# Other places for attention units, a fold, operand buffers, PSUM banks and the last group's turns in a fused attention and MLP kernel

## The chip, the cores and the metric

The kernel runs on one core of a Trainium2 chip. Its time is the device time of one execution in microseconds (us). A core has five engines that run side by side, each in the order of its own instructions: TensorE (PE) multiplies matrices into PSUM banks, VectorE (DVE) and ScalarE (ACT) work on elements, GpSimd (POOL) is hardly used here, SyncE (SP) issues the DMA transfers. They wait for each other by semaphores.

## The reference, cut to what matters

```python
# 8 batches x 576 positions = 4608 tokens, 8 heads of 64; everything is fp32
for each chunk of 64 tokens, each batch and head:
    s = q @ k.T / 8;  s = exp(s - max(s));  p = s / sum(s);  x = p @ v
# x: [4608, 512]
a = x @ w1;  b = x @ w2                 # moe:  512 -> 1024
y = ((a * b) @ w3) @ w_out              #       1024 -> 1024 -> 512
h = y @ w_in                            # moe2: 512 -> 2048
g = max(h, 0) + alpha * min(h, 0)
out = g @ w_out2                        #       2048 -> 512
```

## The kernel before, in words

Every fp32 operand is kept as two rounded halves, HI and LO, and each product is three passes of matmuls (LO x HI, HI x HI, HI x LO). A 128x512 matmul starts every 227 ns in a full stretch.

**First products, blocks b = 0 to 8 of 512 tokens.** A hand-written list starts the kernel (blocks 0 and 1, up to about 139 us). Then comes the loop over `b = 2..8` and `f = 0..7`. A step f has two half-slots of twelve matmuls: `a` into one bank of a pair, copied by ACT, and `b` into the other, multiplied by VectorE with that copy. The product `a*b` goes to DRAM (`g_dram`). Between the half-slots stand the pieces of two attention units of 256 tokens each, for the next block: `unit_parts` puts four pieces of a unit (scores with the row maximum; exponentials, sum and scaling; transposes of the probabilities with their copy `pt` by ACT; product with `v` and the halves of `x`) after the half-slots that the tuple `places` names. In blocks 2 to 7 there are also calls of `convert()`: it splits a piece of a weight into its halves on ACT and VectorE (for moe2 further pieces `wm` are formed and stored). A converted piece of `w3` is later multiplied with `w_out` (`fold`, twelve matmuls into `wc`), so that moe's last two products become one. The order on TensorE is that of the program; on the other engines a scheduler sets it within limits.

**Last product of moe.** Five groups n of two half-blocks of tokens (the first one, s = 4, is half as wide). Each is a Winograd form of Strassen's scheme: seven products o0 to o6 of quarter operands in place of eight. `araw` tiles are read back from DRAM; VectorE and ACT form sums and the halves `op`, in a ring of buffer pairs named in `OPS`; TensorE multiplies them into banks, ACT and VectorE combine the results into `y`. Towards the end of this stage `load_y` and `operand(o)` prepare the operands `yo` of moe2 in the order `ORDER`, at the places that `EARLY` names.

**First product of moe2.** 18 turns of 14 slots, six matmuls a slot, seven products again, each for two column pieces i = 0, 1 (function `both`). A turn uses `a` (two banks) for products 4, 3, 0 and 6 and banks `b`, `c` for 5, 2 and 1. ACT copies the running sum out of `a` at three points (`keep`: p1, u2, v), VectorE adds `b` or `c`, ACT and VectorE apply the leaky step, and the result `r` goes to DRAM. All these tiles share one ring of work buffers, `tmp`. At the last turn of a group s each product's operand is replaced by the next group's (`operand`, one ACT cast and one addition).

**Last product of moe2.** Five groups as in moe. The last group's results are transposed on TensorE, copied by ACT into rows `o`, and stored by SP.

Of the kernel before, what the change touches and what calls it, by code (L numbers as in the profile page):

```python
# [18 lines left out]
P = 128  # L19
TB = 512  # L20
# [33 lines left out]
PAIRS = [(1, 2), (3, 4), (5, 6), (7, 8)]  # L54
# [23 lines left out]
def tile_attention_moe_moe(ctx: ExitStack, tc: tile.TileContext, qkv: bass.AP, w12: bass.AP,  # L78
# [177 lines left out]
    def convert():  # L256

        i = ahead[0]
        if i >= len(conv):
            return  # L260
        ahead[0] = i + 1
        while folds and folds[0] <= i - 2:
            fold(folds.pop(0))
        if conv[i][0] == "m":
            second_weight(i)
            if i % 2:
                combined_weight(i)
        else:
            convert_a(i)
            convert_b(i)  # L270
            convert_a(i + 1)
            convert_c(i)
            convert_d(i)
            convert_e(i)
            folds.append(i)
# [170 lines left out]
    def add(out, x, y, op=ALU.add):  # L446
        vector.tensor_tensor(out=out, in0=x, in1=y, op=op)

    ORDER = (4, 3, 5, 0, 2, 6, 1)
    y_op, ys = {}, {}  # L450

    def load_y(s):
# [115 lines left out]
            moe_weight[at] = [parts[:, a, i] for a in (HI, LO)]  # L568

    CONVERSIONS = {4: 7, 5: 7, 6: 6, 7: 6, 8: 2}  # L570
    pinned[0] = True
    for b in range(2, NB):
        parts = {}
        if b + 1 < NB:
            for i, places in enumerate(((0, 1, 4, 6), (8, 9, 12, 13)) if b < 4 else ((0, 1, 6, 8), (4, 5, 10, 12))):
                parts.update(unit_parts(2 * (b + 1) + i, places))
        for f in range(NF1):
            pa, pb = (bank(n) for n in ("cd" if sets % 2 else "ab"))
            sets += 1
            proj1(b, f, 0, pa)  # L580
            a = tmp("a")
            scalar.copy(a, pa)
            parts.get(2 * f, lambda: None)()
            proj1(b, f, 1, pb)
            product(b, f, a, pb)
            parts.get(2 * f + 1, lambda: None)()
            n = CONVERSIONS.get(b, 0)
            for _ in range(1 + (f in (3, 4)) if b < 4 else n * (f + 1) // NF1 - n * f // NF1 if b < NB - 1 else f < n):
                convert()
            if (b, f) == (3, NF1 - 1):  # L590
                while folds:
                    fold(folds.pop(0))
                load_unit(11)
            if b == NB - 1:
                for at in LOADS[f]:
                    moe_weights(*at)

    EARLY = {2: (-1,), 3: ORDER[:4], 4: ORDER[4:]}
    turns = Counter()

    def copied(out, x):
# [32 lines left out]


    RAWS, SUMS = ("raw0", "raw1", "raw2", "s31"), ("s28", "s29", "s30")
    OPS = (("s16", "s17"), ("s18", "s19"), ("s20", "s21"), ("s22", "s23"))
    NM = NF1 // 4
    groups = (len(PAIRS),) + tuple(range(len(PAIRS)))
    reads = [(s, q, m) for s in groups  # L640
# [10 lines left out]
    for n, s in enumerate(groups):  # L651
        w = wide[s]
        x5, x4, c11, u2 = (post[:, i, :, :w] for i in range(4))
        (b0, c0), (b1, c1) = ((b, 0) for b in PAIRS[s]) if s < len(PAIRS) else ((0, 0), (0, HW))

        def keep_y(b, c, k, x, w=w):
            nc.sync.dma_start(out=y_dram[b][:, k:k + 2, c:c + w], in_=x)

        qa, qc = ("p23", "att") if n % 2 == 0 else ("att", "p23")
        p5, p4 = pair(qa, "q")[:, :, :w], [bank(q)[:, :w] for q in "ab"]  # L660
        sums = []
        for m in range(NM):
            a21, a22 = raw(s, 2, m), raw(s, 3, m)
            sm = slot(cycle("sum", SUMS), "sum", F32)[:, :, :w]
            add(sm, a21, a22)
            sums.append(sm)
            o4 = spread(a22)
            o5 = spread(sm)
            ordered[0] = True
            for f in closing:  # L670
                f()
            closing = []
            multiply(o4, m, 1, p4, m == 0, m == NM - 1)
            multiply(o5, m, 0, p5, m == 0, False)
        p7, p1 = pair(qc, "q")[:, :, :w], [bank(q)[:, :w] for q in "cd"]
        if n == len(PAIRS):
            weights(0, 0)
        for m in range(NM):
            a11, a21 = raw(s, 0, m), raw(s, 2, m)
            add(a21, a11, a21, ALU.subtract)  # L680
            o1 = spread(a11)
            o7 = spread(a21)
            if m == 0:
                for e in range(2):
                    copied(x4[:, e], p4[e])
                copied(x5, p5)
            multiply(o1, m, 4, p1, m == 0, False)
            multiply(o7, m, 2, p7, m == 0, m == NM - 1)
            add(sums[m], sums[m], a11, ALU.subtract)
            o6 = spread(sums[m])  # L690
            if m == 0:
                p6 = [bank(q)[:, :w] for q in "ab"]
            multiply(o6, m, 3, p6, m == 0, m == NM - 1)
        for e in range(2):
            copied(c11[:, e], p1[e])
        if n == len(PAIRS):
            weights(0, 1)
        for m in range(NM):
            a12 = raw(s, 1, m)
            multiply(spread(a12), m, 5, p1, False, m == NM - 1)  # L700
            add(sums[m], a12, sums[m], ALU.subtract)
            multiply(spread(sums[m]), m, 6, p5, False, m == NM - 1)
            if m == 0:
                for e in range(2):
                    add(u2[:, e], p6[e], c11[:, e])
                add(x5, u2, x5)
                add(x5, p7, x5)
                keep_y(b1, c1, 2, x5)
            else:
                add(x4, u2, x4)  # L710
                add(x4, p7, x4)
                keep_y(b1, c1, 0, x4)

        def close(c11=c11, u2=u2, p1=p1, p5=p5, b0=b0, c0=c0, keep_y=keep_y):
            for e in range(2):
                copied(c11[:, e], p1[e])
            keep_y(b0, c0, 0, c11)
            add(u2, p5, u2)
            keep_y(b0, c0, 2, u2)
        closing = [close]  # L720
        for o in EARLY.get(n, ()):
            load_y(0) if o < 0 else operand(o)
    close()
    ordered[0] = False
    for j in range(2, NJ // 2):
        weights(0, j)

    def products(s, j, o, ps, first, last):
        for k in range(2):
# [1 line left out]
                matmul(ps, weight[j, o][a][:, k * P:(k + 1) * P], y_op[s, o][m][:, k],  # L731
                       start=first and k + i == 0, stop=k == 1 and i == 2, skip_group_check=not (first and last))
        if j == NJ - 1 and s + 1 < len(wide):
            operand(o)
    def leaky(s, js, q, h, t):
        w, r = wide[s], tmp("r")[:, :h.shape[1]]
        scalar.activation(out=r, in_=h, func=AF.Relu)
# [14 lines left out]
    for turn, (s, j, jj) in enumerate(passes):  # L752
        if j == (2 if s else 4) and s + 1 < len(wide):
            load_y(s + 1)
        if turn in (0, 1):
            for k in range(2):
                weights(0, 2 * turn + 4 + k)
        a = [bank(n) for n in "ab"]
        p1, u2, v, b, c = ([None] * 2 for _ in range(5))

        def both(i, o, ps, first, last):
            w = wide[s]
            for n, k in enumerate(jj[i]):
                products(s, k, o, ps[:, n * w:(n + 1) * w], first and n == 0, last)

        def keep(name, i):
            t = tmp(name)
# [1 line left out]
            return t  # L769

        def second(i):
            which = (2 * turn + i) % 3
            bc = pair("att" if which == 0 else "p23", "bc") if which != 1 else None
            b[i], c[i] = (bc[:, h] for h in range(2)) if bc is not None else (bank(n) for n in "cd")
            both(i, 5, b[i], True, True)
            add(p1[i], p1[i], b[i])
            leaky(s, jj[i], 0, p1[i], p1[i])
# [1 line left out]
        for i in range(2):  # L779
            both(i, 4, a[i], True, False)  # L780
            p1[i] = keep("p1", i)
        second(0)
        for i in range(2):
            both(i, 3, a[i], False, False)
            u2[i] = keep("u2", i)
        second(1)
        for i in range(2):
            both(i, 0, a[i], False, False)
            v[i] = keep("v", i)
# [21 lines left out]
    def fetch(t, s, q, m):  # L811
        nc.sync.dma_start(out=t, in_=g2_dram[s, q, m])

    def turned(s, c, half, tag, t):

        w = wide[s]
        ps = pair(tag, "tr")
        for i in range(2):
            for e in range(4):
                transpose(ps[:, i, e * P:(e + 1) * P], c[e // 2][:, e % 2, (t + i) * P:(t + i + 1) * P], ident)  # L820
        for i in range(2):
            o = tmp("o")
            scalar.copy(o.rearrange("p (a g c) -> p g a c", a=4, c=32), ps[:, i].rearrange("p (g a c) -> p g a c", a=4, c=32))
            b, r = (PAIRS[s][half], 0) if w == TB else (0, half * w)
            r += b * TB + (t + i) * P
            nc.sync.dma_start(out=out[r:r + P, :], in_=o)

    def rows(s, quads, half, t):

# [17 lines left out]
    for s in range(len(wide)):  # L847
# [48 lines left out]
            copied(c11[:, e], p1[e])  # L896
        for m in range(NM):
            a12 = raw(s, 1, m)
            multiply(spread(a12), m, 5, p1, False, m == NM - 1)
            add(sums[m], a12, sums[m], ALU.subtract)  # L900
            multiply(spread(sums[m]), m, 6, p5, False, m == NM - 1)
            if m == 0:
                for e in range(2):
                    add(u2[:, e], p6[e], c11[:, e])
                add(x5, u2, x5)
            elif m == 1:
                add(x4, u2, x4)
            elif m == 2:
# [6 lines left out]
            add(u2, p5, u2)  # L915
        closing = [close]
        done = [lambda s=s, c=c, h=h, t=t: rows(s, c, h, t) for h, c in ((1, (x4, x5)), (0, (c11, u2))) for t in range(w // P)]
    close()
    for t in range(0, w // P, 2):
        for h, c, q in ((1, (x4, x5), qc), (0, (c11, u2), qa)):  # L920
            turned(s, c, h, q, t)


# [45 lines left out]
```

## Time and profile before

| | |
|---|---|
| median of 3 runs | 1429.05 us (1426.08 to 1432.37) |
| profiled execution | 1429.92 us |
| its span on the trace | 1428.1 us |
| mean granted TensorE clock | 0.998 of full speed |
| TensorE busy | 1379.2 us, 97% of the span |
| VectorE busy | 1088.6 us, 76% |
| ScalarE busy | 767.4 us, 54% |
| blocks 2 to 8 of the first products | about 139 to 546 us |
| moe's last product | 546 to 721 us |
| moe2's first product | 721 to 1076 us |
| moe2's last product, with the stores | 1076 to 1428 us |

TensorE is nearly always busy, so a reader looks for the pauses of TensorE and at what ended each of them: an engine that waits is shown with the time that it sat idle before an instruction and the instruction of another engine that released it.

### The profile page before, as it was taken

Reading aid. Unit: us, or ns where it says so; the run is one execution under the profiler, and the core shown is the slowest. Engines: PE = TensorE matmul, PEld = TensorE weight load, DVE = VectorE, ACT = ScalarE, POOL = GpSimd, SP = SyncE. Lnnn points to the kernel's source line nnn. Section 1 sums busy time; section 2 is a strip of 40 time slices with the busy share of each in tenths; the row PEclk is TensorE's granted clock in tenths of the full one; section 3 lists DMA queues with packets and bytes.
Section 4 is the critical chain, followed back from the end, with each engine's and each line's share of the span. In section 5 each row is a group of like instructions: output and inputs, shape, how many; then the busy total and the mean of one; then the engine's idle time right before and its main releaser. Section 6 shows DMA issues by size and latency. Waiting matters only on the chain.

```text
span 1428.1 us, 23134 instructions
## 1 busy us (share of the span) xinstructions
PE 1379.2 (97%) x8584; PEld 1149.2 (80%) x8584; DVE 1088.6 (76%) x1601; ACT 767.4 (54%) x1597; POOL 9.5 (1%) x22
## 2 busy tenths in 40 slices
PE   5899999999999999999999999999999999999998
PEld 4688778788778889887887787878898888888888
DVE  6889887778877856989855748575667879889785
ACT  6544454554554524454456767687765444444434
POOL 0000000000000000000000000000000000000020
PEclk9999999999999999999999999999999999999999
DMA  8654565699888855566984424332488563635452
GB/s 251 209 177 156 185 242 194 229 324 310 307 296 291 293 216 164 201 219 209 330 297 168 153 106 166 116 134 114 165 315 328 197 216 122 216 133 179 147 152 86
DMA packets 140673, 296.71 MB, mean 208 GB/s; under 512 B 14608, under 2 KB 62224, under 8 KB 140560
## 3 DMA queue, kind: packets, MB, share of 16 engines
q1 hardware_dynamic: 140048, 294.19, 59.7%
q8 instruction: 67, 1.10, 0.3%
q0 software_dynamic: 512, 1.05, 0.2%
q14 instruction: 46, 0.38, 0.1%
HBM read 182.98 MB, written 112.20 MB: 207 GB/s over the span
## 4 chain that ended last, share of the span: by engine, by line
PE 72%; DVE 12%; DMA 6%; ACT 6%; issue 3%; SPq 1%; ACTq 0%; DVEq 0%
PE b L124 15%; PE a L124 14%; PE q L124 14%; PE d L124 10%; PE c L124 9%; PE bc L124 6%; ACT e L70 4%; DVE m L70 3%; PE wc L124 3%; DVE p L70 2%; DMA raw<-in_w 1%; DMA yq<-y_dram 1%; DVE wm L70 1%; PE pa L124 1%; DMA araw<-g_dram 1%
## 5 line engine op out<-in xcount | busy, mean ns | idle before, releaser
L124 PE MATMUL q<-op,w 128*128 128x512 f32 (+1 forms) x960 | 211.8, 368 | 0.0
L124 PEld LDWEIGHTS q<-op,w 128*128 128x128 f32 x960 | 168.5, 189 | 29.9
L70 ACT CAST op<-araw 128x1024 fp32r<-128x1024 f32 (+1 forms) x120 | 115.4, 967 | 117.2 <-PE d L124 37.6
L70 DVE TENSOR_TENSOR op<-araw,op 128x1024 fp32r<-128x1024 f32 (+1 forms) x120 | 132.9, 1113 | 25.4 <-ACT op L70 24.9
L70 ACT CAST op<-sum 128x1024 fp32r<-128x1024 f32 (+1 forms) x90 | 87.0, 967 | 88.9 <-PE q L124 55.0
L70 DVE TENSOR_TENSOR op<-sum,op 128x1024 fp32r<-128x1024 f32 (+1 forms) x90 | 100.2, 1113 | 32.8 <-ACT op L70 32.2
L124 PE MATMUL b<-x,wa 128*128 128x512 f32 x432 | 110.0, 405 | 0.0
L124 PE MATMUL a<-yo,w 128*128 128x512 f32 (+1 forms) x438 | 103.1, 373 | 5.1 <-ACT p L70 3.2
L124 PE MATMUL a<-x,wa 128*128 128x512 f32 x432 | 104.5, 390 | 3.5 <-DVE x L70 3.5
L124 PE MATMUL d<-x,wa 128*128 128x512 f32 x432 | 105.2, 392 | 0.4 <-DVE wa L70 0.4
L124 PE MATMUL c<-x,wa 128*128 128x512 f32 x432 | 104.5, 390 | 0.0
L70 ACT ACTIVATE e<-sc,mx 128x64 f32<-128x64 f32 x288 | 86.0, 361 | 23.8 <-DVE mx L70 23.8
L124 PEld LDWEIGHTS a<-x,wa 128*128 128x128 f32 x432 | 80.7, 188 | 20.5 <-DVE x L70 3.8
L124 PEld LDWEIGHTS b<-x,wa 128*128 128x128 f32 x432 | 81.4, 193 | 17.8
L124 PEld LDWEIGHTS a<-yo,w 128*128 128x128 f32 x438 | 76.9, 188 | 22.2 <-ACT p L70 5.0
L124 PEld LDWEIGHTS c<-x,wa 128*128 128x128 f32 x432 | 80.9, 188 | 16.9
L124 PEld LDWEIGHTS d<-x,wa 128*128 128x128 f32 x432 | 80.2, 188 | 16.8 <-DVE wa L70 0.5
L124 PE MATMUL b<-yo,w 128*128 128x512 f32 (+1 forms) x402 | 91.8, 367 | 0.8 <-ACT t L70 0.8
L124 PE MATMUL c<-op,w 128*128 128x512 f32 (+1 forms) x345 | 89.7, 368 | 0.7 <-DVE op L70 0.7
L124 PE MATMUL bc<-yo,w 128*128 128x512 f32 (+1 forms) x408 | 90.1, 363 | 0.0
L124 PE MATMUL d<-op,w 128*128 128x512 f32 (+1 forms) x345 | 89.6, 368 | 0.0
L124 PE MATMUL a<-op,w 128*128 128x512 f32 (+1 forms) x315 | 81.9, 368 | 1.4 <-DVE op L70 1.4
(143 smaller groups left out, 2505.2 us busy)
## 6 DMA issues: line engine op xcount, KB each, us to landing
araw<-g_dram SPq DMA_DIRECT2D x120, 512.0 KB, 4.1
g_dram<-r SPq DMA_DIRECT2D x144, 256.0 KB, 2.0
w_dram<-wm SPq DMA_DIRECT2D x48, 512.0 KB, 4.6
w<-w_dram SPq DMA_DIRECT2D x48, 512.0 KB, 6.4
qk<-in_qkv SPq DMA_DIRECT2D x36, 512.0 KB, 6.0
g_dram<-a SPq DMA_DIRECT2D x72, 256.0 KB, 3.3
raw<-in_w2nd SPq DMA_DIRECT2D x32, 512.0 KB, 5.3
raw<-in_w SPq DMA_DIRECT2D x16, 512.0 KB, 4.3
```

Of the source, the lines that this page charges most:

```text
L70: ins = f(*args, **kw)
L124: ins = nc.tensor.matmul(*args, **kw)
```

## The change

- `convert()` makes a fold when two are outstanding, and only at a piece of `w3`; the last two folds come in block 4 (f = 0 and 1) rather than at the end of block 3, and the load of unit 11 after them.
- The places of the attention pieces are other ones in block 2 and in blocks 4 to 7.
- `ORDER` is (4, 5, 3, ...); the operands of moe2 are prepared at other points of the last two groups.
- `OPS` has six pairs of buffers, and four again in the last group.
- In moe2's first product, `a` takes banks a, b in even turns and c, d in odd ones; `b` and `c` take the same two pairs in every turn; product 5 of both pieces comes before product 3; an operand is replaced two calls of `both` later.
- In moe2's last group eight transposes (x5, x4) stand ahead of the last two multiplications, copies are divided between ACT and VectorE, and the stores between ACT's and SP's queues.

```diff
@@ convert
-        while folds and folds[0] <= i - 2:
-            fold(folds.pop(0))
         if conv[i][0] == "m":
...
         else:
+            if len(folds) > 1:
+                fold(folds.pop(0))
             convert_a(i)
@@
-    ORDER = (4, 3, 5, 0, 2, 6, 1)
+    ORDER = (4, 5, 3, 0, 2, 6, 1)
@@ loop over blocks
+    PLACES_OF = {2: ((0, 1, 5, 7), (9, 10, 13, 14)), 3: ((0, 1, 4, 6), (8, 9, 12, 13))}
-            for i, places in enumerate(((0, 1, 4, 6), (8, 9, 12, 13)) if b < 4 else ((0, 1, 6, 8), (4, 5, 10, 12))):
+            for i, places in enumerate(PLACES_OF.get(b, ((0, 1, 5, 7), (6, 8, 11, 13)))):
...
-            if (b, f) == (3, NF1 - 1):
-                while folds:
-                    fold(folds.pop(0))
-                load_unit(11)
+            if b == 4 and f < 2:
+                fold(folds.pop(0))
+                if f == 1:
+                    load_unit(11)
@@ moe's last product
-    EARLY = {2: (-1,), 3: ORDER[:4], 4: ORDER[4:]}
+    EARLY = {(3, 2, 0): (-1,), (3, 3, 0): ORDER[:1], (4, 1, 1): ORDER[1:2], (4, 2, 0): ORDER[2:3], (4, 2, 1): ORDER[3:4]}
-    OPS = (("s16", "s17"), ("s18", "s19"), ("s20", "s21"), ("s22", "s23"))
+    OPS = tuple((f"s{n}", f"s{n + 1}") for n in range(12, 24, 2))
+        def early(part, m):
+            for o in EARLY.get((n, part, m), ()):
+                load_y(0) if o < 0 else operand(o)
+        if n == len(PAIRS):
+            OPS = OPS[2:]
+            turns["op"] = 0
...
     close()
+    for o in ORDER[4:]:
+        operand(o)
@@ moe2's first product
         if j == NJ - 1 and s + 1 < len(wide):
-            operand(o)
+            late.append((calls[0] + 2, o))
...
-        a = [bank(n) for n in "ab"]
+        a = [bank(n) for n in ("ab", "cd")[turn % 2]]
...
+            while late and late[0][0] <= calls[0]:
+                operand(late.pop(0)[1])
+            calls[0] += 1
...
         def second(i):
-            which = (2 * turn + i) % 3
-            bc = pair("att" if which == 0 else "p23", "bc") if which != 1 else None
-            b[i], c[i] = (bc[:, h] for h in range(2)) if bc is not None else (bank(n) for n in "cd")
+            bc = pair(("att", "p23")[i], "bc")
+            b[i], c[i] = (bc[:, h] for h in range(2))
...
         second(0)
+        if s < len(PAIRS):
+            second(1)
         for i in range(2):
             both(i, 3, a[i], False, False)
             u2[i] = keep("u2", i)
-        second(1)
+        if s == len(PAIRS):
+            second(1)
@@ moe2's last group
+            final = s == len(PAIRS) and m == NM - 1
+            if not final:
+                multiply(o2, m, 5, p1, False, m == NM - 1)
...
+            if final:
+                tr = pair(qc, "tr")
+                rows1 = [tmp("o") for _ in range(2)]
+                turned(x5, 1, [tr[:, 0], tr[:, 1]], rows1)
+                turned(x4, 0, [bank(q) for q in "ab"], rows1)
+                stored(1, rows1)
+            multiply(o3, m, 6, p5, False, m == NM - 1)
+            if final:
+                multiply(o2, m, 5, p1, False, True)
...
+def turned(x, h, ps, os):     # 4 transposes, then one copy by ACT and one by VectorE
+def stored(half, os):
+        for t in range(2):
+            r = half * HW + t * P
+            (nc.sync if t else nc.scalar).dma_start(out=out[r:r + P, :], in_=os[t])
```

The first place is ACT in block 5, around unit 12's copy `pt` and unit 13's exponentials `e` (x16 stands for sixteen in a row). Before:

```order
L70 COPY a_4115<-a_4101 128x512
L70 CAST wm_4089<-t32_4080 128x512
L70 ACTIVATE m_4192<-raw_3944 128x512
L70 CAST wm_4085<-t14_4079 128x512
L70 ACTIVATE e_3855,sm_4153<-sc_4117,mx_4150 128x64 x16
L70 COPY a_4212<-c_4198 128x512
L70 COPY pt_4223<-pa_4214 128x1024
```

And after the change:

```order
L70 COPY a_4115<-a_4101 128x512
L70 CAST wm_4089<-t32_4080 128x512
L70 ACTIVATE m_4147<-raw_3944 128x512
L70 CAST wm_4085<-t14_4079 128x512
L70 COPY pt_4140<-pa_4131 128x1024
L70 COPY a_4167<-c_4153 128x512
L70 ACTIVATE m_4280<-raw_4071 128x512
L70 CAST wm_4300<-m_4073 128x512
L70 CAST wm_4304<-m_4147 128x256
L70 ACTIVATE e_3869,sm_4205<-sc_4169,mx_4202 128x64 x8
```

The copy stood behind the sixteen exponentials and one product copy; it now stands ahead of all of them.

The second place is VectorE in block 2, where the low half of a piece of `w3` is finished (`w3_2263` before, `w3_2198` now: the same piece) and unit 7's softmax is scaled (`e_1877`). Before:

```order
L70 TENSOR_SCALAR p_2301<-m_2264 128x512
L70 TENSOR_SCALAR m_2298<-m_2298 128x512
L70 TENSOR_TENSOR wm_2284<-m_2099,wm_2284 128x512
L70 SCALAR_TENSOR_TENSOR p_2301<-raw_2097,p_2301 128x512
L70 TENSOR_TENSOR m_2264<-m_2264,w3_2263 128x512
L70 TENSOR_TENSOR a_2320<-d_2307,a_2320 128x512
L70 TENSOR_TENSOR w3_2263<-m_2264,p_2301 128x512
```

And after the change:

```order
L70 TENSOR_TENSOR m_2199<-m_2199,w3_2198 128x512
L70 TENSOR_TENSOR w3_2198<-m_2199,p_2248 128x512
L70 TENSOR_SCALAR sm_2184<-sm_2184 128x16
L70 RECIPROCAL sm_2184<-sm_2184 128x16
L70 TENSOR_TENSOR a_2267<-d_2254,a_2267 128x512
L70 TENSOR_TENSOR e_1877<-e_1877,sm_2184 128x1024
L70 TENSOR_TENSOR t14_2314<-wf_2312 128x256
```

Before, the scaling of `e_1877` and the pieces of the combined weight stood ahead of the rows shown, 29 rows before the weight; now the weight is finished four rows ahead of that scaling.

The third place is ACT at the start of moe2's first product (its first turn, in the order of every turn). Before:

```order
L70 COPY p1_7550<-a_7542 128x512
L70 COPY p1_7558<-b_7543 128x512
L70 ACTIVATE r_7568<-p1_7550 128x512
L70 COPY u2_7579<-a_7542 128x512
L70 ACTIVATE p1_7550<-p1_7550 128x512
L70 COPY u2_7587<-b_7543 128x512
L70 ACTIVATE r_7598<-p1_7558 128x512
L70 COPY v_7609<-a_7542 128x512
```

And after the change:

```order
L70 COPY p1_7550<-a_7542 128x512
L70 COPY p1_7558<-b_7543 128x512
L70 ACTIVATE r_7568<-p1_7550 128x512
L70 ACTIVATE p1_7550<-p1_7550 128x512
L70 ACTIVATE r_7581<-p1_7558 128x512
L70 COPY u2_7592<-a_7542 128x512
L70 ACTIVATE p1_7558<-p1_7558 128x512
L70 COPY u2_7600<-b_7543 128x512
```

The first copy `u2` of a turn had one relu pass between it and the copies `p1`; it now has three, all over `p1` of the two column pieces.

## Rows read from the trace of the kernel before

**Rows 1.** The page, busy time of each engine, its share of the span, instructions.

```profile
PE 1379.2 (97%) x8584; PEld 1149.2 (80%) x8584; DVE 1088.6 (76%) x1601; ACT 767.4 (54%) x1597; POOL 9.5 (1%) x22
```

**Rows 2.** Waits of TensorE: for what, us in all, times, longest.

```profile
PE pa L124 <- ACT pt L70: 12.5, 7, 2.9
PE pa L129 <- DVE e L70: 7.2, 4, 3.4
...
PE wc L124 <- DVE w L70: 5.0, 2, 2.7
...
PE a L124 <- ACT p L70: 3.2, 3, 1.2
PE a L124 <- ACT t L70: 1.8, 4, 0.5
PE a L124 <- DVE op L70: 1.4, 1, 1.4
PE b L124 <- ACT t L70: 1.1, 4, 0.3
PE c L124 <- DVE op L70: 0.7, 1, 0.7
```

**Rows 3.** Windows: length, busy PE, PEld, DVE, ACT, POOL; clock, DMA share, GB/s.

```profile
195.00:215.00 20.00, 17.28 (x194) 13.72 (x192) 19.45 (x38) 9.55 (x16) 0.00 (x0) 1.00 0.83 274
...
360.00:380.00 20.00, 17.85 (x135) 14.50 (x134) 17.14 (x35) 13.18 (x47) 0.00 (x0) 0.91 0.92 320
420.00:440.00 20.00, 17.35 (x133) 14.13 (x133) 15.39 (x31) 13.01 (x46) 0.00 (x0) 0.91 0.75 263
```

**Rows 4.** Timeline of TensorE, blocks 5 and 6: start, us, line, operation, [idle before <-releaser].

```profile
372.45 1.16 PE L124 MATMUL pa<-pt,v 64*64 64x64 f32 x64 [2.15 <-ACT pt L70]
...
427.38 1.31 PE L124 MATMUL pa<-pt,v 64*64 64x64 f32 x64 [2.65 <-ACT pt L70]
```

**Rows 5.** Timeline of TensorE, block 2.

```profile
156.03 1.06 PE L129 MATMUL pa<-ident,e 128*128 128x128 f32 x8 [1.92 <-DVE e L70]
...
200.53 2.56 PE L124 MATMUL wc<-wo,w 128*128 128x512 f32 x10 [2.72 <-DVE w L70]
```

**Rows 6.** Timeline of ACT, block 5.

```profile
366.15 0.31 ACT L70 ACTIVATE e<-sc,mx 128x64 f32<-128x64 f32 x1 [2.37 <-DVE mx L70]
...
371.27 1.13 ACT L70 COPY pt<-pa 128x1024 f32<-128x1024 f32 x1
```

**Rows 7.** Timeline of VectorE, block 5.

```profile
371.53 1.23 DVE L70 TENSOR_TENSOR e<-e,sm 128x1024 f32<-128x1024 f32 x1
...
393.71 1.22 DVE L70 TENSOR_TENSOR x<-pa,x 128x1024 fp32r<-128x1024 f32 x1
```

**Rows 8.** Timeline of TensorE, block 5, unit 13.

```profile
357.13 1.16 PE L124 MATMUL sc<-qk 64*64 64x64 f32 x64
...
387.17 1.16 PE L124 MATMUL pa<-pt,v 64*64 64x64 f32 x64
```

**Rows 9.** Timeline of TensorE, moe2's first product: a boundary turn, a plain turn.

```profile
806.30 1.65 PE L124 MATMUL a<-yo,w 128*128 128x512 f32 x6 [0.90 <-ACT p L70]
...
825.49 1.52 PE L124 MATMUL a<-yo,w 128*128 128x512 f32 x6
826.85 1.52 PE L124 MATMUL b<-yo,w 128*128 128x512 f32 x6
```

**Rows 10.** Timeline of ACT, moe2's first product: a boundary turn, a plain turn.

```profile
794.62 1.06 ACT L70 CAST yo<-yq 128x1024 fp32r<-128x1024 f32 x1 [0.97 <-PE d L124]
...
805.66 0.59 ACT L70 COPY p<-a 128x512 f32<-128x512 f32 x1 [1.02 <-DMA g_dram<-r]
...
828.41 0.59 ACT L70 COPY u<-b 128x512 f32<-128x512 f32 x1 [0.24 <-PE b L124]
```

**Rows 11.** Timeline of TensorE and SP's queue, the end.

```profile
1421.17 2.10 PE L129 MATMUL tr<-ident,post 128*128 128x128 f32 x16
...
1422.86 1.90 SPq L826 DMA_DIRECT2D out<-o  x4
```

More of the change, by code (lines that the diff above doesn't have):

```diff
@@ L674, in tile_attention_moe_moe @@
             multiply(o5, m, 0, p5, m == 0, False)
+            early(1, m)
         p7, p1 = pair(qc, "q")[:, :, :w], [bank(q)[:, :w] for q in "cd"]
@@ L693, in tile_attention_moe_moe @@
             multiply(o6, m, 3, p6, m == 0, m == NM - 1)
+            early(2, m)
         for e in range(2):
@@ L712, in tile_attention_moe_moe @@
                 keep_y(b1, c1, 0, x4)
+            early(3, m)
         def close(c11=c11, u2=u2, p1=p1, p5=p5, b0=b0, c0=c0, keep_y=keep_y):
@@ L720, in tile_attention_moe_moe @@
         closing = [close]
-        for o in EARLY.get(n, ()):
-            load_y(0) if o < 0 else operand(o)
     close()
+    for o in ORDER[4:]:
+        operand(o)
     ordered[0] = False
@@ L726, in tile_attention_moe_moe @@
         weights(0, j)
+    late, calls = [], [0]
     def products(s, j, o, ps, first, last):
@@ L812, in fetch @@
         nc.sync.dma_start(out=t, in_=g2_dram[s, q, m])
[L814 to L826, printed above, removed]
+    def turned(x, h, ps, os):
+        for t in range(2):
+            for e in range(2):
+                n = (2 * h + e) * P
+                transpose(ps[t][:, n:n + P], x[:, e, t * P:(t + 1) * P], ident)
+        for t in range(2):
+            to, ps_t = (y.rearrange(f, a=4, c=32)[:, 2 * h:2 * h + 2]
+                        for y, f in ((os[t], "p (a g c) -> p g a c"), (ps[t], "p (g a c) -> p g a c")))
+            (vector.tensor_copy if t else scalar.copy)(to, ps_t)
+    def stored(half, os):
+        for t in range(2):
+            r = half * HW + t * P
+            (nc.sync if t else nc.scalar).dma_start(out=out[r:r + P, :], in_=os[t])
     def rows(s, quads, half, t):
@@ L898, in tile_attention_moe_moe @@
             a12 = raw(s, 1, m)
-            multiply(spread(a12), m, 5, p1, False, m == NM - 1)
+            o2 = spread(a12)
+            final = s == len(PAIRS) and m == NM - 1
+            if not final:
+                multiply(o2, m, 5, p1, False, m == NM - 1)
             add(sums[m], a12, sums[m], ALU.subtract)
-            multiply(spread(sums[m]), m, 6, p5, False, m == NM - 1)
+            o3 = spread(sums[m])
+            if final:
[7 more added lines that the diff above has]
+                multiply(o2, m, 5, p1, False, True)
             if m == 0:
@@ L905, in tile_attention_moe_moe @@
                 add(x5, u2, x5)
+            elif s == len(PAIRS):
+                if m == 1:
+                    add(x4, u2, x4)
+                    add(x5, p7, x5)
+                    add(x4, p7, x4)
             elif m == 1:
@@ L917, in tile_attention_moe_moe @@
         done = [lambda s=s, c=c, h=h, t=t: rows(s, c, h, t) for h, c in ((1, (x4, x5)), (0, (c11, u2))) for t in range(w // P)]
[L918 to L921, printed above, removed]
+    add(u2, p5, u2)
+    for e in range(2):
+        (vector.tensor_copy if e else scalar.copy)(c11[:, e], p1[e])
+    rows0 = [tmp("o") for _ in range(2)]
+    turned(u2, 1, [bank(q) for q in "ab"], rows0)
+    tr = pair(qc, "tr")
+    turned(c11, 0, [tr[:, 0], tr[:, 1]], rows0)
+    stored(0, rows0)
 def kernel(**inputs):
```

## The prediction

> **What bounds the kernel now.** I read the page's busy line first: TensorE is busy for 1379.2 us of the 1428.1 us span [rows 1]. The change neither adds nor removes matmuls, apart from eight transposes that go ahead of the last product, so the time can only move through TensorE's pauses. The waits of TensorE are therefore the second view [rows 2]. Most of the first three rows there belongs to the first 140 us, whose hand-written list is not touched. What the change can reach is: one wait of 1.92 us for a softmax [rows 5], both waits of a fold for its weight (5.0 us together) [rows 2], two waits of a values product for the copied probabilities (2.15 and 2.65 us) [rows 4], the two for `op` (1.4 and 0.7), and the rows for `p` and `t` (3.2, 1.8 and 1.1) that all lie in moe2's first product [rows 2]. The third view is the granted clock by stretch. The two 20 us windows that hold the waits of 2.15 and 2.65 us read 0.91, the one that holds a fold's wait reads 1.00 [rows 3]. At half speed for some 3.6 us of a window, 9% of 20 us is lost: 1.8 us more for each of the two.
>
> The Trainium skill, "TensorE: Matmul & The Clock Gate", section "HAM oscillation", has it that idle gaps take the clock down to half and that the penalty is paid again each time. Rows 3 and 4 agree for two waits, and the fold's wait of 2.72 us [rows 5], longer than either, cost no clock. So by the rule a pause costs itself or itself and 1.8 us, and which is not read from its length alone; I use this only for the price of new waits, below.
>
> **Part 1, attention units in blocks 4 to 7 (from 292 us to 502 us).** ACT runs in order. In block 5 the copy `pt` of unit 12 started at 371.27, behind the sixteen exponentials of unit 13, of which the first started at 366.15 [rows 6]; unit 12's values product then began at 372.45, late by 2.15 [rows 4]. The order shows the copy ahead of the exponentials now, since unit 12's turn comes one half-slot earlier and unit 13's scores two later. Unit 14 in block 6 is the same case. The gain is 2.15 + 2.65, and 2 x 1.8 of clock: 8.4 us.
>
> What is late next is the second unit of the block. Its probabilities were ready at 371.53 + 1.23 = 372.76 [rows 7], 14.5 us after its scores product ended (357.13 + 1.16) [rows 8]. From scores to turn there are now five half-slots of 2.72 us (twelve matmuls, two slots as in [rows 9]) and one values product of 1.16, 14.8 us: ready with 0.3 us to spare. But between maximum and multiply VectorE has fifteen other operations now, the first unit's `x` of 1.22 us among them, where it had seven, so I take 1.0 us of waiting in block 5, where the queue is longest, and bound it by 0 and 2.4 (two of `x`). Then its values product ends two half-slots (5.44 us) before the next block's first matmul, where it was three (8.16). In block 5 the low half of `x` was finished at 393.71 + 1.22 = 394.93 [rows 7], 6.6 us after the values (387.17 + 1.16) [rows 8]. With an unchanged queue that is 1.2 us late. Three more boundaries have the same places. I take 2.5 us for all new waits of this part, mostly block 5's (1.0 + 1.2). The bounds are 0 (the freed ACT also frees VectorE) and 4 x (1.2 + 1.0 + 1.8), each with its share of half clock: 16.
>
> **Part 2, the fold.** In block 2 a fold stood 2.72 us for `w` [rows 5]; its twin in block 3 has the rest of the 5.0 [rows 2]. VectorE made that weight behind a softmax and the pieces of the combined weight. The order puts the weight (`w3_2198`) ahead of the softmax now, and each fold takes a weight that has been ready for one conversion. Both waits go: 5.0 us. The two folds that leave the end of block 3 are issued in block 4: the same 24 matmuls, at no cost. The load of unit 11 moves past them on SP; its wait on the second fold holds up the rows behind it on that queue, which are not needed for six half-slots, so I take 0, bounded by 0 and 2. Unit 6's turn in block 2 goes behind the next half-slot (2.72 us), which covers its wait of 1.92 [rows 5]: 1.9 us. Its second unit goes one place later, with the fold (2.72) and a half-slot between its values and block 3: 5.44 us. The weight conversions there are ahead by then, so 0 is taken, within the bound of part 1.
>
> **Part 3, moe's last product.** Six pairs of operand buffers for four. ACT's casts into `op` wait less for TensorE to release a pair, so VectorE's second half is earlier. The two waits of TensorE are 1.4 + 0.7 us [rows 2], and the additions of `load_y` still stand ahead of the first. I take 1.5, between 0 (the chain is VectorE's own) and 2.1.
>
> **Part 4, moe2's first product.** A slot is six matmuls, 1.36 us (825.49 to 826.85) [rows 9], a turn 14 slots. The waits for `t` come where a turn's first slot needs the bank that ACT is still reading for the turn before; with two bank pairs by turns they go. The waits for `p` come where the seventh slot needs a bank whose copy `u` is behind. At 794.62 a cast for the next operands had itself stood 0.97 us for TensorE, and at 805.66 the copy `p` had stood 1.02 us for a store of `r`, whose buffer it takes over [rows 10]. The casts now come two slots later, when their buffer is free. The price is that in every turn the copy `u` must end in one slot (1.36), where it had two, since both second products stand together. Worked out for a plain turn: the third slot ends at 4.08, addition and both relu passes fill ACT to 6.1 (each 512-column pass near the copy's 0.59, an estimate) [rows 10]; the second relu ends at 6.8, when the fifth slot ends too; the copy takes 0.59 to 7.4; the seventh slot starts at 8.16. That leaves 0.7 us. Of 3.2 + 1.8 + 1.1 = 6.1 [rows 2] I take 5.0, as the four turns at a change of group keep seven casts; bounds 6.1 and, in the slower rival, a loss.
>
> **Part 5, the last group.** After the last product came 16 transposes in 2.10 us from 1421.17 and four stores in line, issued from 1422.86 on [rows 11], up to 1428.1. Eight transposes (1.05) now stand ahead of the last product, and two copies run side by side. That removes the second eight's copies and two issues of about 0.5 us (1.90 for 4) from the end and adds 1.05 in front: a gain of 0.7, bounded by -1.0 and 1.5. The Trainium skill, "DMA: Bandwidth & Descriptors", section "Issuing engines are not separate DMA queues", says that stores issued from two engines run on the same 16 DMA engines, and only issue time is saved. No row here has a store on ACT's queue; by the rule the gain is the issue time that I count and nothing for the transfer.
>
> **Sum.** 8.4 + 5.0 + 1.9 + 1.5 + 5.0 + 0.7 - 2.5 = 20.0 us. The profiled execution took 1429.92, so it becomes 1409.9; the median of the three runs shown is 0.87 lower, 1429.05, which makes 1409.0.
>
> **Rivals.** First, VectorE sets the pace. It is the busiest engine beside TensorE in these blocks, and the second unit is pushed against the block's end four times. If the waits reach their bound, 16 instead of 2.5, the time is 1409.0 + 13.5 = 1422.5; at half of it, 1416. For it speaks the 6.6 us of block 5; against it, that VectorE was idle for 2.86 of the 20 us around unit 12's wait [rows 3].
>
> Second, the change does not do what it says: the waits in moe's last product and in moe2's boundary turns are ACT's total work, not buffers or banks. Then parts 3 and 4 give nothing: 1409.0 + 6.5 = 1415.5. For it speaks that seven casts of about 1.06 us enter one turn whatever the banks, and that the wait for the store of `r` stays [rows 10]; against, that ACT idles in front of them.
>
> Third, slower: the copy `u` misses its one slot in every turn of moe2's first product. The place is the seventh and eighth slots, the price per turn what a boundary turn paid for `p`, 0.90 [rows 9], twice. Over 17 turns this is 30.6 us, against 15.0 from the other parts: 1429.05 - 15.0 + 30.6 = 1444.7. It decides the sign from 15.0 / 17 = 0.9 us per turn on. Against it stand the 0.7 us to spare and that in a plain turn the copy `u` waited 0.24 us for TensorE, not the other way [rows 10].
>
> **How the numbers follow.** The forecast, 1409.0, has 0.65, with its own range from 1403 (bounds of parts 3 to 5 reached, no new waits) to 1414. The first rival has 0.16, the second 0.13, the slower one 0.06. The range to hold 8 in 10 goes from 1402 to 1422. A difference of 0.5%, 7.1 us, is about what a measurement of this kernel can tell from none. Faster by more (below 1421.9): the forecast, the second rival and most of the first, 0.86. Within it: the bad end of the first and a mild form of the third, 0.09. Slower: 0.05.
>
> **What would show it.** Right: in the changed kernel's waits of TensorE the rows for `pt`, `w` and `e` past 140 us are gone, the windows of blocks 5 and 6 read 1.00, and moe2's first product takes about 5 us less. A wait of a block's first matmul for `x`, or of a second turn for `e`, above 2.5 us in all shows the first rival; waits for `p`, `u` or `t` in plain turns, the third; waits for `op` as before, the second. The forecast is wrong if the waits go and the time does not, for then another engine was the bound.

## The result and the profile after

The changed kernel takes 1413.05 us (median of 4 runs, 1411.34 to 1416.75) against 1430.3 of the kernel before in the same runs: ratio 0.9887, 95% interval 0.9855 to 0.9919, faster by 1.1%. Its profiled execution took 1411.34 us with a span of 1409.6, 18.5 less than before; 20.0 were forecast. The median lies 4 us above the forecast of 1409.0, inside the forecast's own range (1403 to 1414).

The waits of TensorE after the change, as in [rows 2]: for what, us in all, times, longest.

```profile
PE pa L124 <- ACT pt L70: 7.2, 5, 2.9
...
PE a L124 <- DVE x L70: 5.8, 3, 2.6
PE pa L129 <- DVE e L70: 5.6, 3, 3.6
PE a L124 <- ACT u L70: 2.1, 3, 1.2
PE a L124 <- DVE op L70: 0.9, 2, 0.7
PE c L124 <- DVE op L70: 0.4, 1, 0.4
```

The waits for `w`, `p` and `t` are gone, those for `pt` in blocks 5 and 6 too (five are left, all in the first 140 us). New are three for `u` in moe2's first product and, in block 5, one for `e` and one for `x`. Two of those for `u` (1.23 and 0.41) stand in the first turn after a change of group, here called a boundary turn; the third (0.51) stands in the third turn, a plain one, where VectorE had stood 4.85 us for the load of the next group's operands. A second execution of the same kernel also has one wait for `p`, 1.89 us, in the last turn. The timeline of TensorE in block 5, to be laid beside [rows 4]:

```profile
371.97 1.06 PE L129 MATMUL pa<-ident,e 128*128 128x128 f32 x8 [1.13 <-DVE e L70]
...
382.38 2.88 PE L124 MATMUL d<-x,wa 128*128 128x512 f32 x12
387.20 4.24 PE L124 MATMUL a<-x,wa 128*128 128x512 f32 x12 [1.93 <-DVE x L70]
```

The last row's twelve matmuls are busy for 4.24 us against 2.88 for the twelve above: half clock after the wait. The windows that hold the two waits, columns as in [rows 3]:

```profile
360.00:380.00 20.00, 18.87 (x146) 15.35 (x145) 17.98 (x37) 12.70 (x46) 0.00 (x0) 1.00 0.92 308
380.00:400.00 20.00, 18.07 (x132) 14.19 (x131) 14.82 (x28) 10.27 (x43) 0.00 (x0) 0.91 0.80 267
```

The stages, from the first matmul of each to that of the next in either trace; two folds (5.4 us) went from block 3 to block 4:

| stage | before | after | difference |
|---|---|---|---|
| to block 2 (not changed) | 139.0 | 137.6 | -1.4 |
| block 2 | 72.1 | 66.9 | -5.2 |
| block 3 | 80.4 | 72.4 | -8.0 |
| block 4 | 50.6 | 56.2 | +5.6 |
| block 5 | 54.5 | 54.1 | -0.4 |
| block 6 | 54.8 | 52.3 | -2.5 |
| blocks 7 and 8 | 94.1 | 94.1 | 0.0 |
| moe, last product | 175.2 | 173.9 | -1.3 |
| moe2, first product | 354.9 | 349.7 | -5.2 |
| moe2, last product and stores | 352.5 | 352.4 | -0.1 |

The first row is scatter between executions: the same instructions start block 2 between 136.8 and 141.3 us in the fourteen traces of this study. Other stages scatter too where their code is the same: moe's last product took 174.8 to 175.2 us in the four traces with its old code and 173.1 to 175.1 in the ten with the new one; moe2's first product 354.0 to 355.1 in three with the old code and 348.6 to 351.2 in seven with the new one.

### The profile page after: what moved, and what is told of

Same layout as the page of the kernel before. It is cut to its first block, busy times and chain, and to the rows that moved or that the text cites. A ratio compares the mean times of both kernels' runs of the same rounds, so it can differ in the third digit from the quotient of the medians.

```text
span 1409.6 us, 23169 instructions
## 1 busy us (share of the span) xinstructions
PE 1375.6 (98%) x8584; PEld 1148.5 (81%) x8584; DVE 1089.6 (77%) x1606; ACT 763.7 (54%) x1596; POOL 9.5 (1%) x22
## 3 DMA queue, kind: packets, MB, share of 16 engines
q0 software_dynamic: 512, 1.05, 0.2%
## 4 chain that ended last, share of the span: by engine, by line
PE 83%; DVE 7%; ACT 4%; DMA 3%; issue 2%; SPq 0%; DVEq 0%; ACTq 0%
PE q L124 14%; PE a L124 14%; PE c L124 13%; PE b L124 13%; PE d L124 13%; PE bc L124 10%; PE wc L124 3%; ACT e L70 2%; DVE m L70 2%; DMA raw<-in_w 1%; DVE op L70 1%; PE pa L124 1%; DVE p L70 1%; PE sc L124 1%; DMA araw<-g_dram 1%
## 5 line engine op out<-in xcount | busy, mean ns | idle before, releaser
L124 PE MATMUL bc<-yo,w 128*128 128x512 f32 (+1 forms) x600 | 132.6, 368 | 0.0
L124 PEld LDWEIGHTS bc<-yo,w 128*128 128x128 f32 x600 | 105.2, 189 | 18.7
L124 PE MATMUL a<-x,wa 128*128 128x512 f32 x432 | 108.6, 401 | 5.8 <-DVE x L70 5.8
L124 PE MATMUL b<-x,wa 128*128 128x512 f32 x432 | 105.1, 392 | 0.0
L124 PE MATMUL b<-op,w 128*128 128x512 f32 (+1 forms) x315 | 81.8, 368 | 0.0
L70 ACT ACTIVATION_READ_ACCUMULATOR e<-sc,mx 128x1 f32 x288 | 71.0, 249 | 0.0
```

The source lines that it names most:

```text
L70: ins = f(*args, **kw)
L124: ins = nc.tensor.matmul(*args, **kw)
```

## The experiments

Theory: TensorE's waits add up; each removed is worth its length (and its half clock, where there is one), and what the change pays are block 5's two waits. Rivals: VectorE's total work or ACT's is the bound and waits only move.

**Parts 1 and 2 alone** (`convert()`, folds, all attention places on the kernel before).

> The kernel before with the change's edits to convert(), the folds and the attention places alone (parts 1 and 2 of the prediction). Theory (each wait removed is worth its own length, and block 5's new waits are all that is paid): the waits for e in block 2 (1.9), for w (5.0), for pt in blocks 5 and 6 (4.8) and two stretches at half clock (3.6) go, 15.3 us; new are a wait of a turn for e of about 1.1 us and one for x of about 1.9 us with some 1.5 us of half clock, as in the changed kernel: -10.8 us against before, 1419. Rival (VectorE's total work sets the blocks' pace, so waits only move): less than half of that, 1424 or more, with other waits in blocks 4 to 7.

Measured: 1419.47, ratio 0.9928 (0.9904 to 0.9951), 10.8 us less. TensorE's timeline of this kernel, block 5:

```profile
375.93 1.06 PE L129 MATMUL pa<-ident,e 128*128 128x128 f32 x8 [1.38 <-DVE e L70]
391.02 4.60 PE L124 MATMUL a<-x,wa 128*128 128x512 f32 x12 [1.79 <-DVE x L70]
```

The same two waits, with half clock again (4.60). The theory's number holds; the rival's 5.4 us or less is outside the interval (7.0 to 13.7).

**Part 1 alone**, the places of blocks 4 to 7.

```diff
-... if b < 4 else ((0, 1, 6, 8), (4, 5, 10, 12))
+... if b < 4 else ((0, 1, 5, 7), (6, 8, 11, 13))
```

> The kernel before with the attention places of blocks 4 to 7 alone (folds and block 2 as before). Theory: the two waits for pt (4.8) and their half clock (3.6) go, and block 5 pays a wait for e (1.1 to 1.5) and one for x (1.5 to 1.9), sometimes with half clock behind the latter (1.5): -3.5 to -6 us against before, 1423 to 1426. Rival (the folds that the change moves into block 4 are needed, since they give VectorE 5.4 us there): more waits for x, at the end of block 4 as well, and no gain.

Measured: 1427.0, ratio 0.9986 (0.9970 to 1.0003): 2 us, and zero is not excluded. In its trace block 5 pays 1.89 for `e` and 2.34 for `x`, block 4 only 0.31 for `x`. Blocks 4 to 6 took 157.1 us against 159.9 before: 2.8 less, about the 2.7 that the changed kernel gains there once its two folds are taken off. The profiled execution is nevertheless one of the slowest of its ten (1432.35 us), because TensorE fell to half clock behind both fold waits in blocks 2 and 3, whose code this kernel does not change (last section); those two blocks took 158.3 us against 152.5. So part 1 is worth 2 to 3 us rather than the 3.5 to 6 expected, and the folds in block 4 are no condition of it: the rival's wait there is small.

**Part 4 alone**, moe2's first product.

> The kernel before with the edits to moe2's first product alone (bank pairs by turns, fixed banks for b and c, both second products together, operands two calls later). Theory: the waits for p and t (6.1 us) go, and waits for u of about 2 us in the first turn of a group take a part back, as in the changed kernel: -4 us, 1426, seen in the trace rather than in the time. Rival (the gain there needs the other operand order and the earlier loads): waits for p or t of 3 us or more stay.

Measured: 1428.29, ratio 0.9994 (0.9973 to 1.0016), which tells nothing of 4 us. The trace does: that stage took 351.0 us (354.9 before), with no wait for `p` or `t` and 2.6 for `u`. That is 3.9 us less, as the theory says.

**The delay of two calls taken out.**

```diff
-            late.append((calls[0] + 2, o))
+            late.append((calls[0], o))
```

> The changed kernel without the delay of two calls before an operand of moe2's first product is replaced. Theory (ACT, strictly in order, stands behind a cast whose buffer TensorE still reads): ACT's casts wait for TensorE again (near 1 us each in a boundary turn), and the waits of TensorE for u in boundary turns grow from 2.1 in all to 4 to 6: +3 us. Rival (banks and not the delay made the gain): same time within 1 us.

Measured: 1414.69 against 1410.61 of the changed kernel on the same chip, ratios 0.9909 (0.9894 to 0.9924) and 0.9880 (0.9863 to 0.9897). ACT's timeline and then TensorE's, without the delay:

```profile
777.35 1.05 ACT L70 CAST yo<-yq 128x1024 fp32r<-128x1024 f32 x1 [1.19 <-PE bc L124]
```

```profile
771.50 1.66 PE L124 MATMUL c<-yo,wx 128*128 128x512 f32 x6 [0.98 <-ACT u L70]
...
792.57 1.65 PE L124 MATMUL a<-yo,w 128*128 128x512 f32 x6 [0.95 <-ACT u L70]
```

Casts stand for TensorE on ACT's queue again, and TensorE then waits 5.7 us in all for ACT's copies `u`, and 0.9 for VectorE's additions to `u`. The intervals touch, but the stage shows it: 355.0 us without the delay, 351.0 in the changed kernel's execution beside it, and 354.9 before the change. So beside the other edits of part 4 the delay is worth 4 us. The bank pairs and the joined order without it remove the waits for `t` and `p`, but others for `u` take their place and the stage gains nothing. The delay without the bank pairs was not run.

**The joined second products taken apart** (`second(1)` behind the copies `u` again).

> The changed kernel with moe2's second product of the second piece back behind the copies u (the order before), banks and delay as changed. Theory (the banks and the delay make the gain; the joined second products cost a plain turn nothing, having 0.7 us to spare): no waits in plain turns either way; the waits for u in boundary turns (1.6 to 2.1) fall, those for p come back at most in their place: within 1.5 us of the changed kernel. Rival (the joined order is the gain): 3 us or more of waits for p or t come back.

Measured: 1414.59, ratio 0.9901 (0.9885 to 0.9917); the kernel with all stores of the end on SP (below), which differs from the changed one only at its end, took 1412.64 in the same rounds. Waits for `p` of 4.1 us come back, the 2.1 for `u` go:

```profile
792.16 2.93 PE L124 MATMUL a<-yo,w 128*128 128x512 f32 x6 [2.37 <-ACT p L70]
```

Six matmuls busy for 2.93 us are at half clock, and the window around them reads 0.91, 1.8 us lost:

```profile
785.00:805.00 20.00, 17.63 (x72) 14.14 (x71) 14.33 (x18) 12.36 (x23) 0.00 (x0) 0.91 0.52 175
```

The rival was right on the waits: 4.1 us of them come back, 2 more than go. The stage took 351.7 us against 349.7 in that other kernel, but without the half clock it would be about 349.9, and the last section shows that the half clock comes and goes with the same code. So what the joined order is worth, up to 2 us, is not settled: this is one trace, and the intervals of the times overlap. In a plain turn of this trace the order before does not wait either.

**Four calls of delay**, with block 5's edit below.

> The changed kernel with block 5's second values product one half-slot earlier and operands of moe2's first product replaced four calls later in place of two. Theory (ACT's casts crowd the boundary turn, so spreading them further helps): the waits for u (1.6 to 2.1) fall under 0.7, 1407. Rival (what holds there is the ring of work buffers, each waiting for a store of r to land, 1.7 us in the run before): the waits stay, 1408.8 as with block 5's edit alone.

Measured: 1409.59, ratio 0.9867 (0.9853 to 0.9882). The waits for `u` stay: 1.22 and 0.48, against 1.23 and 0.49 with block 5's edit alone. ACT's timeline in the same turn, of the changed kernel and of this one:

```profile
787.69 0.63 ACT L70 ACTIVATE r<-u 128x512 f32<-128x512 f32 x1 [1.71 <-DMA g_dram<-r]
```

```profile
787.50 0.63 ACT L70 ACTIVATE r<-u 128x512 f32<-128x512 f32 x1 [1.72 <-DMA g_dram<-r]
```

ACT stands for a store whose work buffer it takes over, as it did before the change [rows 10]. In the changed kernel's other boundary turn with a wait, ACT stood 0.89 us for a store and TensorE 0.41 for `u`; in both turns TensorE's wait is 0.48 us shorter than ACT's. The rival is supported: the ring of work buffers, not the casts, holds the boundary turn. It is not shown by a change of the ring, for a larger one was not tried.

**One conversion less in block 5.**

```diff
-    CONVERSIONS = {4: 7, 5: 7, 6: 6, 7: 6, 8: 2}
+    CONVERSIONS = {4: 7, 5: 6, 6: 7, 7: 6, 8: 2}
```

> The changed kernel with one conversion of block 5 moved to block 6 (CONVERSIONS 7, 6, 7, 6, 2 in place of 7, 7, 6, 6, 2). Theory (VectorE's queue in block 5 makes the two waits left there): some eleven VectorE operations, 5 to 6 us, leave block 5, so its waits for e (1.1) and x (1.9) and the half clock behind the latter (about 1.5) go: -4.5 us against the changed kernel, 1408.5. Rival (the two waits are set by the places, the softmax chain and the 5.44 us between values and the next block): they stay at 2 us or more. Second rival: the waits move to block 6, same time.

Measured: 1412.68, ratio 0.9880 (0.9854 to 0.9906): nothing gained. The wait for `e` is 0.58, that for `x` 2.21. VectorE's waits from 375 to 390 us:

```profile
DVE t L70 <- DMA g_dram<-a: 3.9, 1, 3.9
```

With less work VectorE stood 3.9 us for the store of a product `a`, whose buffer its next operation takes over. So work alone does not make the late `x`; the ring and a store's landing do here. VectorE's timeline has the same in the same place in the changed kernel and in the one with all stores of the end on SP, which runs block 5 with the same code:

```profile
380.84 0.43 DVE L70 TENSOR_SCALAR p<-m 128x512 uint32<-128x512 uint32 x1 [1.20 <-DMA g_dram<-a]
```

```profile
381.83 0.43 DVE L70 TENSOR_SCALAR p<-m 128x512 uint32<-128x512 uint32 x1 [2.35 <-DMA g_dram<-a]
```

TensorE's wait for `x` was 1.93 us in the first and 3.08 in the second. In all six executions that run blocks 4 to 6 with this code, VectorE stood 0.6 to 2.35 us for that store, and the wait for `x` was longer than that by 0.70 to 0.73. So the store sets how late `x` is, and about 0.7 us is left to the places and VectorE's queue. A store is not the only way to a late `x`: with part 1 alone it came 2.34 us late without such a wait of VectorE.

**Block 5's stores on GpSimd's queue.**

```diff
-        nc.sync.dma_start(out=g_dram[b, h, m // 2][:, m % 2], in_=a)
+        (nc.gpsimd if b == 5 else nc.sync).dma_start(...)
```

> The changed kernel with the eight stores of block 5's products issued on GpSimd's queue in place of SP's; every compute engine's order is the same. In the changed kernel VectorE stood 1.2 us (3.9 and 2.5 us in the two variants) at the end of block 5 for such a store, whose buffer the next operation takes over. Theory (the late x is a late store, queued behind 512 KB loads on SP): that wait of VectorE goes, the wait for x falls from 1.9 to 0.7 or less, no half clock behind it, -2 to -3 us against the changed kernel. Rival (the 16 DMA engines are full, whichever queue; or VectorE has the work anyway): the store lands as late, the wait for x stays near 1.9.

Measured: 1416.08, ratio 0.9909 (0.9893 to 0.9926): slower than the changed kernel's 1410.61, though the intervals touch. DMA issues of block 5, with KB and median us to landing:

```profile
g_dram<-a POOLq DMA_DIRECT2D x7, 256.0 KB, 5.8
```

On SP's queue it was 4.5 for eight. Now ACT stands for a store, and TensorE's turn for `e`; ACT's timeline and TensorE's:

```profile
356.14 0.69 ACT L70 ACTIVATE m<-raw 128x512 f32<-128x512 f32 x1 [3.48 <-DMA g_dram<-a]
```

```profile
376.22 1.94 PE L129 MATMUL pa<-ident,e 128*128 128x128 f32 x8 [4.13 <-DVE e L70]
```

The theory fails: the stores land later than before, by 1.3 us, and the wait for `x` is 2.35. The rival has these two about right, but not the wait for `e`. Block 5 takes 59.1 us against 53.7 in the changed kernel beside it. The two waits are 3.9 us longer; most of the rest is half clock behind the first, in which the eight transposes took 1.94 us for 1.06. ACT's wait for the store is shown; that it lengthens TensorE's wait for `e` is the likeliest reading, since nothing else was changed. Whether SP's order or the load of the DMA engines delays them on SP stays open.

**Block 5's second values product one half-slot earlier**, then the same beside the changed kernel itself.

```diff
+    PLACES_OF = {5: ((0, 1, 5, 7), (6, 8, 11, 12)), 2: ...}
```

> The changed kernel with the values product of block 5's second unit one half-slot earlier (places 6, 8, 11, 12). Theory: the wait for e stays (1.1), the wait for x (1.9) and its half clock go since x has 8.16 us and stands four rows earlier on VectorE, with 0.3 us of it left at most: -3 us against the changed kernel, 1410. Rival: the values product now waits for pt by as much as x gains.

> The changed kernel unaltered, on the chip of the next three, so that they are compared with it side by side. Expected 1412 to 1414. A theory that the half clock behind a wait depends on where the wait falls, not on its length, expects the wait for x at the end of block 5 (1.9 before) again, with or without half clock behind it.

> Block 5's second values product one half-slot earlier, again, five rounds: theory that it is really faster than the changed kernel: 2 to 3 us less than that in the same rounds. Rival: the earlier 1409.5 was scatter, and both are the same within 1 us, since in its trace the wait for e grew by as much as the wait for x shrank.

Measured: 1409.51, ratio 0.9861 (0.9834 to 0.9887). Then, in the same rounds, 1408.80, ratio 0.9865 (0.9850 to 0.9879), beside 1410.61, ratio 0.9880 (0.9863 to 0.9897), of the changed kernel. In the trace of the first the wait for `x` was 0.89, in that of the second none is left; the wait for `e` was 1.51 and 0.98, and block 6 has another of 1.36 and 0.75. All three medians with this edit (the one with four calls of delay is the third) lie 1.0 to 1.8 us below the lower of the changed kernel's two, but the intervals overlap: it beats the kernel before by 1.35%, and whether it beats the changed one is not settled.

**All stores of the end on SP.**

```diff
-            (nc.sync if t else nc.scalar).dma_start(...)
+            nc.sync.dma_start(...)
```

> The changed kernel with all four stores of the last group on SP's queue. Theory (only issue time is saved by a second queue): from the last copy of rows to the end the trace shows 0.3 to 0.6 us more, one issue. Rival (the queues carry the transfers side by side): 1.5 us more or over. Neither can be told from the time, only from the trace's end.

Measured: 1412.64. From the start of the last product's last matmul to the end it is 5.74 us, and 5.75 with two queues: neither theory's number; the second queue saves not even an issue. From the last copy of rows, which the expectation names, it is 3.96 us in both.

## Why the prediction was right, and where a term was not

- **Waits for `w` and `e` in blocks 2 and 3.** Forecast 6.9 us, measured 5.2 + 8.0 - 5.4 = 7.8. Both waits of the fold are gone; the order on VectorE was the reason. Counted from the start of block 2, the fold that had waited started at 58.0 us before and at 54.6 after, its weight was finished at 61.5 before and at 46.8 after.
- **Block 5 and 6.** The gain came: the two waits for `pt` are gone, with their half clock. Block 7, which waits for nothing, took 50.6 us; blocks 5 and 6 were 8.1 us above twice that before, so the gain was 8.1 where 8.4 were counted. The term "2.5 us for all new waits" is the mis-sized one: blocks 4 to 6 gave -0.4 - 2.5 + (5.6 - 5.4) = -2.7 us, so what is new cost 5.4. The waits themselves were 1.13 and 1.93 for the 1.0 and 1.2 counted; left out of the value taken, though not of its bound, was the half clock behind the second, 1.7 us by block 6's length. These make 4.8; the last 0.6 lies in blocks 4 and 5 and I can't place it. The window 380 to 400 reads 0.91, where 1.00 was to be the sign of a right forecast. I had put the cause of the late `x` in VectorE's queue of work; the runs show that its larger part is a store that had not landed.
- **`op`.** Forecast 1.5, stage 1.3, which is partly luck: by the means of the ten traces with the new code and the four with the old one it is 0.7 (174.3 against 175.0), and part 3 was not run alone.
- **moe2's first product.** Forecast 5.0, stage 5.2. Plain turns wait for nothing but the 0.51 us in the third one, so the 0.7 us to spare held elsewhere, and the slower rival did not come. That the boundary turns keep something was forecast; the runs point to the ring as what holds them. Which edit gave it was forecast in part only: the casts' delay is needed for the whole gain, and the bank pairs and the joined order do not give it without the delay.
- **The end.** Forecast 0.7, stage 0.1, but that stage took 351.5 to 353.2 us in the fourteen traces and can't tell. From the start of the last matmul to the end it was 7.06 us before and is 5.75 after, 1.3 less; the eight transposes moved ahead (1.05) leave 0.3 of it. The issue time that I counted as saved by the second queue is not there.
- **The rivals.** By the sign that was set for the first one, waits for `x` and `e` above 2.5 us in all, it shows: they were 3.06. It has its place, block 5, and a third of its price, but a store's landing has the larger part in the wait for `x`, not VectorE's pace. The second rival, that parts 3 and 4 give nothing, is refuted for part 4 by the stage in seven traces; for part 3, 0.7 us of 1.5 is left.

## What to carry to other kernels

On an engine that runs in order, look at what stands ahead of the instruction that TensorE waits for (a copy behind sixteen exponentials, a cast whose buffer is still read) and move it where its own operands are early. Count a ring's buffers among the waits: a tile that is stored is free only when its store has landed, and this can look like an engine with too much work. Price a wait of TensorE as its length and, at times, the clock on top: mostly 1.8 us here, once 3.4 (next section).

## What the runs showed of the hardware

A wait's length did not decide whether the clock fell to half after it. The wait for `x` at the end of block 5 came in many of these kernels. In the changed kernel 1.93 us of it were followed by half clock, in the kernel with all stores on SP 3.08 were not. TensorE's row and the window of that kernel:

```profile
388.19 3.01 PE L124 MATMUL a<-x,wa 128*128 128x512 f32 x12 [3.08 <-DVE x L70]
```

```profile
380.00:400.00 20.00, 16.92 (x133) 13.55 (x132) 14.73 (x28) 9.13 (x37) 0.00 (x0) 1.00 0.76 254
```

And the fold's wait in block 2, after which the clock had stayed at full speed in the kernel before [rows 3, 5], was followed by half clock with the same code and nearly the same length in the kernel with part 1 alone; its row and window:

```profile
201.09 4.63 PE L124 MATMUL wc<-wo,w 128*128 128x512 f32 x10 [2.60 <-DVE w L70]
```

```profile
195.00:215.00 20.00, 17.40 (x122) 13.64 (x121) 16.67 (x33) 8.55 (x15) 0.00 (x0) 0.83 0.79 264
```

A window of 20 us at 0.83 has lost 3.4 us, twice the 1.8 us that the prediction counts behind a wait [rows 3].

So one profiled execution's half clock is not a property of the code. The Trainium skill, "TensorE: Matmul & The Clock Gate", section "What's actually happening", says that the activity is judged in a free-running window that does not start with the kernel; these rows agree in that the same code and nearly the same wait end either way, and no run here shows the window itself. That the half clock comes and goes may be one reason why executions of one kernel differ by several us. It is why a part worth 4 us was read here from its stage rather than from the median, and why a stage too has to be searched for half clock before two are compared.
